# A shorter accumulating DMA with a fifth transpose group, later transposes in the first bodies, and a rearranged start in a fused dynamic convolution and two-matmul kernel

## The chip, the cores and the metric

One core of a Trainium2 chip runs the kernel. The metric is the device time of one execution in microseconds. Each run has a profile of one execution (its span is 1.7 to 2.1 us shorter than that execution's time) and, where rounds are given, repeated times beside the kernel before on the same chip. Three words recur. *Landing* is the moment at which all of a DMA's data is in place. The *slow clock* is a stretch in which the profile shows a granted TensorE clock of about half. A *one-off gap* is a stretch in which TensorE stands without waiting for anything that the profile names; where these gaps lie is told under e11.

## The reference, cut to what matters

```python
# attention part: x (8, 4096, 192), weight_gen (8, 4096, 8 heads, 7 taps)
w = exp(weight_gen - max); w = w / sum(w)          # softmax over the 7 taps
out[b,s,h,g] = sum_k w[b,s,h,k] * x[b, s-6+k, h*24+g]
# second part, on the 32768 x 192 result
h = x @ w_in          # 192 x 2048
g = h - tanh(h)
return g @ w_out      # 2048 x 192
```

## The kernel before

The kernel works on 32 blocks of 1024 tokens. For each block GpSimd multiplies x by the softmax weights, one product per tap, into three tiles: `even` (taps 0, 2, 4), `odd` (1, 3, 5) and `last` (6). An accumulating DMA adds `odd` to `even`. TensorE then transposes and adds up the four groups that are left (three of `even`, and `last`) by matmuls against an identity; ScalarE copies the result out of PSUM as `convT`.

```python
    def products(n, on_vector=()):
        ...
        for k in range(K):
            eng = nc.vector if k in on_vector else nc.gpsimd
            eng.tensor_mul(dst[k]..., x_t[:, k : k + J, :]..., wsm[:, :, :, k : k + 1]...)
            if k == K - 2:
                nc.gpsimd.dma_start(
                    out=even[:]..., in_=odd[:]...,
                    accum_op=mybir.AluOpType.add, max_dma_last_dim=3072)
        prods_of[n] = [even[:, i] for i in range(NPAIR)] + [last[:]]
```

The main loop interleaves, in program order of each engine, the two matmuls of neighbouring blocks with the transposes of the next block and the products of the block after that. A *body* is one pass of the outer loop, a *pair* one pass of the inner one.

```python
    for n in range(NTOT):
        if n + 3 < NTOT: load(n + 3)
        if n + 2 < NTOT: products(n + 2)
        for p in range(J):
            gemm1(n, 2 * p); gemm1(n, 2 * p + 1)      # tanh on ScalarE, subtraction on VectorE
            ...
            if n >= 1: gemm2((n - 1) * J + p)
            if n + 1 < NTOT:
                if p == (2 if n else 5): conv(n + 1, (0, 1))     # transposes of chunks 0 and 1
                if p == (5 if n else 6): conv(n + 1, (2,))       # and of chunk 2
            ...
```

The transposes use the same ring of three PSUM tiles as the first matmul (`tag="ph"`).

The softmax here doesn't subtract the row's maximum and nothing guards it: scores larger than these inputs give would overflow.

## Time and profile before

| what | before |
|---|---|
| time, first three runs | 808.31 us (807.36 to 809.03) |
| TensorE's body | 23.12 us |
| GpSimd's period | 22.74 us |
| accumulating DMA, issue to landing | 10.1 us |
| block 5: issue of its accumulating DMA / first transpose | 137.74 / 152.16 us |

Read it as two machines running in step: GpSimd with its DMA makes a block every 22.74 us, TensorE uses one every 23.12. The page's group rows give the unit costs. Columns: line, engine, operation, names, count, then busy us and mean ns of one, then idle time before them and its releasers:

```profile
L153 POOL TENSOR_TENSOR odd<-x_t,wsm 128x1536 bf16<-128x1536 f32 x92 | 268.5, 2919 | 0.0
L161 POOL DMA_DIRECT2D even<-odd x32 | 41.5, 1298 | 10.0 <-POOL odd L153 9.4
even<-odd POOLq DMA_DIRECT2D x32, 1152.0 KB, 10.1
```

A product costs GpSimd 2.9 us. Issuing the accumulating DMA costs it 1.30 us. The last row is of the DMA issues: 1152 KB each, 10.1 us from issue to landing.

### The profile page before, as it was taken

Reading aid. Unit: us, or ns where it says so; the run is one execution under the profiler, and the core shown is the slowest. Engines: PE = TensorE matmul, PEld = TensorE weight load, DVE = VectorE, ACT = ScalarE, POOL = GpSimd, SP = SyncE. Lnnn points to the kernel's source line nnn. Section 1 sums busy time; section 2 is a strip of 40 time slices with the busy share of each in tenths; the row PEclk is TensorE's granted clock in tenths of the full one; section 3 lists DMA queues with packets and bytes.
Section 4 is the critical chain, followed back from the end, with each engine's and each line's share of the span. In section 5 each row is a group of like instructions: output and inputs, shape, how many; then the busy total and the mean of one; then the engine's idle time right before and its main releaser. Section 6 shows DMA issues by size and latency. Waiting matters only on the chain.

```text
span 805.8 us, 31480 instructions
## 1 busy us (share of the span) xinstructions
PE 737.1 (91%) x14336; PEld 566.7 (70%) x14336; DVE 661.5 (82%) x591; ACT 643.4 (80%) x865; POOL 713.0 (88%) x297
## 2 busy tenths in 40 slices
PE   0066999999999999999999999999999999999997
PEld 0034777777777777777777777777777777777777
DVE  3867688888888888888888888888888888888883
ACT  0066788888888888888888888888888888888883
POOL 5999999999999999999999999999999999996000
PEclk9999999999999999999999999999999999999999
DMA  8794555676655655676565656775655667634112
GB/s 148 230 187 85 114 161 156 166 180 180 179 141 126 149 159 156 172 181 179 138 170 131 149 154 163 180 171 139 176 118 157 153 169 180 168 61 100 43 41 81
DMA packets 30068, 118.66 MB, mean 147 GB/s; under 512 B 4672, under 2 KB 9328, under 8 KB 25784
## 3 DMA queue, kind: packets, MB, share of 16 engines
q0 software_dynamic: 15376, 39.32, 30.6%
q1 hardware_dynamic: 14560, 77.34, 27.4%
q8 instruction: 112, 1.84, 0.9%
q14 instruction: 20, 0.16, 0.1%
HBM read 54.49 MB, written 25.17 MB: 99 GB/s over the span
## 4 chain that ended last, share of the span: by engine, by line
PE 76%; DVE 11%; POOL 5%; ACT 4%; DMA 3%; issue 1%; SPq 0%; POOLq 0%; DVEq 0%
PE ph L205 36%; PE po L236 35%; DVE gt L216 9%; ACT th L214 4%; PE pc L182 4%; POOL even L153 2%; POOL odd L153 2%; DMA x_t<-in_x_dram 1%; DVE odd L153 1%; PE po L277 1%; DMA even<-odd 1%; POOL last L153 0%; POOL wsm L137 0%; POOL even L161 0%; DVE even L153 0%
## 5 line engine op out<-in xcount | busy, mean ns | idle before, releaser
L216 DVE TENSOR_TENSOR gt<-ph,th 128x1024 bf16<-128x1024 f32 x512 | 602.8, 1220 | 106.7 <-ACT th L214 103.3
L214 ACT ACTIVATE th<-ph 128x1024 f32<-128x1024 f32 x512 | 500.3, 1022 | 64.0 <-PE ph L205 60.4
L205 PE MATMUL ph<-convT,w_in 64*128 64x512 bf16 x3072 | 391.9, 378 | 17.2 <-DVE gt L216 16.0
L236 PEld LDWEIGHTS <-gt 64*128 64x128 bf16 x7936 | 344.4, 94 | 52.8 <-ACT th L214 1.7
L236 PE MATMUL po<-w_out,gt 64*128 64x192 bf16 x7936 | 374.1, 243 | 1.7 <-ACT th L214 1.3
L153 POOL TENSOR_TENSOR even<-x_t,wsm 128x1536 bf16<-128x1536 f32 x95 | 281.8, 2967 | 14.2 <-DMA x_t<-in_x_dram 7.1
L153 POOL TENSOR_TENSOR odd<-x_t,wsm 128x1536 bf16<-128x1536 f32 x92 | 268.5, 2919 | 0.0
L205 PEld LDWEIGHTS <-w_in 64*128 64x128 bf16 x3072 | 170.3, 94 | 135.6 <-issue 44.9
L153 POOL TENSOR_TENSOR last<-x_t,wsm 128x1536 bf16<-128x1536 f32 x31 | 105.9, 3415 | 0.0
L261 ACT ACTIVATE out_sb<-po 128x192 f32<-128x192 f32 x248 | 82.0, 331 | 18.5 <-PE po L236 12.2
L192 ACT ACTIVATE convT<-pc 128x1024 bf16<-128x1024 f32 x64 | 51.7, 810 | 47.6 <-PE pc L182 43.5
L182 PE MATMUL pc<-ident,even 64*128 64x64 bf16 x2304 | 46.6, 193 | 45.9 <-DMA even<-odd 45.6
L182 PEld LDWEIGHTS <-even 64*128 64x128 bf16 x2304 | 43.7, 97 | 46.7 <-issue 46.4
L161 POOL DMA_DIRECT2D even<-odd x32 | 41.5, 1298 | 10.0 <-POOL odd L153 9.4
L137 POOL TENSOR_TENSOR wsm<-e_t,zr 128x448 f32<-128x448 f32 x32 | 46.3, 1446 | 0.0
L116 ACT ACTIVATE e_t<-wg_t 128x448 f32<-128x448 f32 x32 | 18.5, 578 | 20.3 <-DMA wg_t<-in_weight_gen_dram 20.3
L126 DVE TENSOR_REDUCE zsum<-e_t 128x64 f32<-128x448 f32 x32 | 19.5, 610 | 10.8 <-ACT e_t L116 10.8
L182 PE MATMUL pc<-ident,last 64*128 64x64 bf16 x768 | 23.4, 193 | 0.0
L153 DVE TENSOR_TENSOR odd<-x_t,wsm 128x1536 bf16<-128x1536 f32 x4 | 15.0, 3782 | 9.6 <-DMA x_t<-in_x_dram 9.6
L130 DVE RECIPROCAL zr<-zsum 128x64 f32<-128x64 f32 x32 | 17.7, 553 | 3.4 <-DVE zsum L126 0.5
L182 PEld LDWEIGHTS <-last 64*128 64x128 bf16 x768 | 17.3, 97 | 0.0
L277 PE MATMUL po<-w_out,gt 64*128 64x192 bf16 x256 | 11.0, 243 | 0.0
(15 smaller groups left out, 31.5 us busy)
## 6 DMA issues: line engine op xcount, KB each, us to landing
even<-odd POOLq DMA_DIRECT2D x32, 1152.0 KB, 10.1
x_t<-in_x_dram SPq DMA_DIRECT2D x24, 1344.0 KB
out_dram<-out_sb SPq DMA_DIRECT2D x31, 768.0 KB
x_t<-in_x_dram SPq DMA_DIRECT2D x8, 1176.0 KB
wg_t<-in_weight_gen_dram SPq DMA_DIRECT2D x32, 224.0 KB
x_t<-in_x_dram SPq DMA_DIRECT2D x8, 157.5 KB
w_in<-in_moe_w_in_dram POOLq DMA_DIRECT2D x8, 96.0 KB, 11.0
w_in<-w_in SPq DMA_DIRECT2D x1, 768.0 KB
```

Source lines behind the costliest of these rows:

```text
L126: nc.vector.reduce_sum(out=zsum[:], in_=e_t[:].rearrange("p j h k -> p (j h) k"), axis=AX.X)
L137: nc.gpsimd.tensor_mul(wsm[:].rearrange("p j h k -> p (j h) k"), e_t[:].rearrange("p j h k -> p (j h) k"), zr[:].rearrange("p (n o) -> p n ...
L153: eng.tensor_mul(dst[k].rearrange("p c j h g -> p j h c g"), x_t[:, k : k + J, :].rearrange("p j (h c g) -> p j h c g", h=H, c=NC), wsm[:, ...
L161: nc.gpsimd.dma_start(out=even[:].rearrange("p i c j h g -> p (i c j h g)"), in_=odd[:].rearrange("p i c j h g -> p (i c j h g)"), accum_o ...
L182: nc.tensor.matmul(pc[:, r, col : col + R], lhsT=prods[k][r * R : (r + 1) * R, c, 2 * j : 2 * j + 2].rearrange("p j h g -> p (j h g)"), rh ...
L192: nc.scalar.activation(out=convT[:, c0 : c0 + nch, :].rearrange("p c (j r t) -> p r (c j) t", r=2, t=R), in_=pc[:, :, 0 : nch * JH * R].re ...
L205: nc.tensor.matmul(ph[:, r, :], lhsT=w_in[r * R : (r + 1) * R, c, f * P : (f + 1) * P], rhs=convT[r * R : (r + 1) * R, c, :], start=(c == ...
L214: last_act[0] = nc.scalar.activation(out=th[:], in_=ph_f, func=ACT.Tanh)
L216: nc.vector.tensor_sub(gt[:], ph_f, th[:])
L236: mm = nc.tensor.matmul(po[:, 0:D], lhsT=g_of[n][f][r * R : (r + 1) * R, col : col + P], rhs=w_out[r * R : (r + 1) * R, f, :], start=(r == ...
L261: last_act[0] = nc.scalar.activation(out=out_sb[:, j, :], in_=po[:, 0:D], func=ACT.Copy)
L277: nc.tensor.matmul(po[:, r, 0:D], lhsT=g_of[n][f][r * R : (r + 1) * R, col : col + P], rhs=w_out[r * R : (r + 1) * R, f, :], start=(f == 0 ...
```

## The change

Its intent: shorten the start, in which TensorE has nothing to do, and keep TensorE from standing at the transposes of the first blocks. The accumulating DMA's row of 4608 elements per partition (3 runs of 1536 in the built kernel) is cut to 4096 (2 runs of 2048); the 512 elements left over become a fifth group of transposes for chunk 2.

```diff
+    ACC = NPAIR * J * D - J * R
...
                 nc.gpsimd.dma_start(
-                    out=even[:].rearrange("p i c j h g -> p (i c j h g)"),
-                    in_=odd[:].rearrange("p i c j h g -> p (i c j h g)"),
+                    out=even[:].rearrange("p i c j h g -> p (i c j h g)")[:, 0:ACC],
+                    in_=odd[:].rearrange("p i c j h g -> p (i c j h g)")[:, 0:ACC],
                     accum_op=mybir.AluOpType.add,
-                    max_dma_last_dim=3072,
+                    max_dma_last_dim=4096,
                 )
+            if k in hooks:
+                hooks[k]()
-        prods_of[n] = [even[:, i] for i in range(NPAIR)] + [last[:]]
+        groups = [even[:, i] for i in range(NPAIR)] + [last[:]]
+        prods_of[n] = [groups + ([odd[:, NPAIR - 1]] if c == NC - 1 else []) for c in range(NC)]
... (conv runs over a list of steps, with the fifth group for chunk 2 alone)
     load(0)
-    for h in range(H):
-        nc.gpsimd.dma_start(out=w_in[h * GC : (h + 1) * GC], ...)
     softmax_exp(0)
     softmax_norm(0)
-    products(0, on_vector=(1, 3, 5, 6))
-    nc.sync.dma_start(out=w_in[R:P], in_=w_in[0:R])
+    products(0, on_vector=(1, 3, 4, 5, 6), hooks={-1: load_w_in})   # w_in after wsm, copied in two halves
     load(1)
-    nc.gpsimd.dma_start(out=w_out[:], ...)
...
-    products(1, on_vector=(2, 5))
+    products(1, hooks={3: load_w_out})
...
-                if p == (2 if n else 5):
+                if p == (2 if n > 3 else 7):
                     conv(n + 1, (0, 1))
-                if p == (5 if n else 6):
+                if p == (5 if n > 3 else 7):
                     conv(n + 1, (2,))
```

Three parts will be told apart below: the *start*, the *DMA* (with its fifth group), and the *late transposes* (bodies 0 to 3).

More of the change, by code (lines that the diff above doesn't have):

```diff
@@ L131, in softmax_norm, with products @@
         zr_of[n] = (e_t, zr)
-    def products(n, on_vector=()):
+    def products(n, on_vector=(), hooks={}):
         x_t = x_of.pop(n)
@@ L150, in products @@
         dst[K - 1] = last[:]
+        if -1 in hooks:
+            hooks[-1]()
         for k in range(K):
@@ L176, in conv @@
         pc = psum_h.tile([P, 2, HT], FP32, name="pc", tag="ph")
-        for k in range(NPAIR + 1):
-            for ci, c in enumerate(chunks):
-                for j in range(JH):
-                    col = (ci * JH + j) * R
-                    for r in range(2):
-                        nc.tensor.matmul(
-                            pc[:, r, col : col + R],
-                            lhsT=prods[k][r * R : (r + 1) * R, c, 2 * j : 2 * j + 2].rearrange(
-                                "p j h g -> p (j h g)"
-                            ),
-                            rhs=ident[r * R : (r + 1) * R, r * R : (r + 1) * R],
-                            start=(k == 0 and ci == 0 and j == 0),
-                            stop=(k == NPAIR and ci == nch - 1 and j == JH - 1),
-                        )
+        steps = [
+            (gi, ci, c)
+            for gi in range(NPAIR + 2)
+            for ci, c in enumerate(chunks)
+            if gi < len(prods[c])
+        ]
+        for si, (gi, ci, c) in enumerate(steps):
+            for j in range(JH):
+                col = (ci * JH + j) * R
+                for r in range(2):
+                    nc.tensor.matmul(
+                        pc[:, r, col : col + R],
+                        lhsT=prods[c][gi][r * R : (r + 1) * R, c, 2 * j : 2 * j + 2].rearrange(
+                            "p j h g -> p (j h g)"
+                        ),
+                        rhs=ident[r * R : (r + 1) * R, r * R : (r + 1) * R],
+                        start=(si == 0 and j == 0),
+                        stop=(si == len(steps) - 1 and j == JH - 1),
+                    )
         c0 = chunks[0]
@@ L301, with load_w_out, load_w_in @@
     ctx.enter_context(tc.manual_schedule())
-    load(0)
-    for h in range(H):
-        nc.gpsimd.dma_start(
-            out=w_in[h * GC : (h + 1) * GC],
-            in_=moe_w_in[h * G : (h + 1) * G].rearrange("(c g) f -> g c f", c=NC),
-        )
+    def load_w_out():
+        nc.gpsimd.dma_start(out=w_out[:], in_=moe_w_out.rearrange("(c p) e -> p c e", c=NFT))
+    def load_w_in():
+        for h in range(H):
+            nc.gpsimd.dma_start(
+                out=w_in[h * GC : (h + 1) * GC],
+                in_=moe_w_in[h * G : (h + 1) * G].rearrange("(c g) f -> g c f", c=NC),
+            )
+        for q in range(2):
+            nc.sync.dma_start(
+                out=w_in[R + q * R // 2 : R + (q + 1) * R // 2],
+                in_=w_in[q * R // 2 : (q + 1) * R // 2],
+            )
+    load(0)
     softmax_exp(0)
     softmax_norm(0)
-    products(0, on_vector=(1, 3, 5, 6))
-    nc.sync.dma_start(out=w_in[R:P], in_=w_in[0:R])
+    products(0, on_vector=(1, 3, 4, 5, 6), hooks={-1: load_w_in})
     load(1)
-    nc.gpsimd.dma_start(out=w_out[:], in_=moe_w_out.rearrange("(c p) e -> p c e", c=NFT))
     softmax_exp(1)
```

## The prediction

> **What bounds the kernel now.** I read the page first (busy shares, the chain's shares), then the chain in order of time, then the timelines of GpSimd and TensorE up to 180 us, then busy time and DMA traffic by stretch.
>
> ```profile
> PE 737.1 (91%) x14336; PEld 566.7 (70%) x14336; DVE 661.5 (82%) x591; ACT 643.4 (80%) x865; POOL 713.0 (88%) x297
> PE 76%; DVE 11%; POOL 5%; ACT 4%; DMA 3%; issue 1%; SPq 0%; POOLq 0%; DVEq 0%
> ```
>
> Two engines are nearly full. TensorE carries the chain, but GpSimd's 88% is an average over a span in which it starts late and stops at 737 us, so it has hardly a gap while it works. The chain in order of time shows who hands over to whom:
>
> ```profile
> 69.52 10.52 DMA even<-odd
> 80.17 1.81 PE pc L182 x64
> 81.99 2.21 PE ph L205 x12
> ...
> 104.89 0.93 PE pc L182 x64
> 105.83 1.43 PE ph L205 x12
> ```
>
> Up to 80 us the chain is load, products on GpSimd and one accumulating DMA; from 80.17 on it is TensorE, with short passages through ScalarE and VectorE. The same 64 transposes take 1.81 us at 80.17 and 0.93 us at 104.89, and the 12 matmuls after them 2.21 against 1.43: TensorE had stood idle 3.62 us and ran slowly afterwards, which cost 0.88 + 0.78 = 1.7 us. Now the two rhythms, TensorE's transposes of chunks 0 and 1 and GpSimd's issues of the accumulating DMA:
>
> ```profile
> 80.17 1.39 PE L182 MATMUL pc<-ident,even 64*128 64x64 bf16 x48 [3.62 <-DMA even<-odd]
> ...
> 104.71 0.88 PE L182 MATMUL pc<-ident,even 64*128 64x64 bf16 x48
> ...
> 127.83 0.88 PE L182 MATMUL pc<-ident,even 64*128 64x64 bf16 x48
> ...
> 152.16 0.88 PE L182 MATMUL pc<-ident,even 64*128 64x64 bf16 x48
> ```
>
> ```profile
> 46.76 1.30 POOL L161 DMA_DIRECT2D even<-odd  x1 [0.30 <-POOL even L153]
> ...
> 69.52 1.30 POOL L161 DMA_DIRECT2D even<-odd  x1 [0.31 <-POOL odd L153]
> ...
> 137.74 1.30 POOL L161 DMA_DIRECT2D even<-odd  x1 [0.30 <-POOL odd L153]
> ```
>
> TensorE repeats every 23.12 us (104.71 to 127.83; the next step is 24.33 because of a 0.93 us gap marked "issue"). GpSimd repeats every 22.74 us ((137.74 - 69.52) / 3). GpSimd gains only about 0.4 us a body on TensorE. The issues at 46.76 and 137.74 serve blocks 1 and 5; at the median 10.1 us to landing, block 5 lands at 147.8, and TensorE asks for it at 152.16. The slack is 4.3 us. So TensorE bounds the steady state with GpSimd close behind, and any plan that moves TensorE earlier meets GpSimd's products after 4.3 us.
>
> The start:
>
> ```profile
> 14.68 10.51 DVE L153 TENSOR_TENSOR odd<-x_t,wsm 128x1536 bf16<-128x1536 f32 x3 [9.57 <-DMA x_t<-in_x_dram]
> ...
> 31.84 1.76 DVE L153 TENSOR_TENSOR even<-x_t,wsm 128x1536 bf16<-128x1536 f32 x1 [1.16 <-POOL wsm L137]
> 33.52 4.46 DVE L153 TENSOR_TENSOR odd<-x_t,wsm 128x1536 bf16<-128x1536 f32 x1
> ```
>
> ```profile
> 2.00:8.00 6.00, 0.00 (x0) 0.00 (x0) 1.17 (x2) 0.60 (x2) 5.48 (x10) 1.00 0.93 177
> 8.00:14.00 6.00, 0.00 (x0) 0.00 (x0) 0.00 (x0) 0.00 (x0) 0.00 (x0) 1.00 1.10 200
> 22.00:26.00 4.00, 0.00 (x0) 0.00 (x0) 4.00 (x2) 0.58 (x1) 4.00 (x2) 1.00 1.03 426
> 70.00:79.70 9.70, 5.25 (x85) 4.03 (x81) 6.77 (x7) 5.00 (x7) 9.62 (x5) 1.00 0.87 157
> ```
>
> The last two columns are the DMA engines' busy share and GB/s. The first x tile lands only at 14.6 us, because the casting load of w_in shares the engines (full from 2 to 14 us at under 200 GB/s). The second x tile, alone at 22 to 26, runs at 426 GB/s: 1.34 MB in about 3.5 us. VectorE's product takes 1.76 us when it goes first and 4.46 when it has to let one of GpSimd's (2.87) pass: the two alternate, they do not overlap.
>
> **What the Trainium skill says.** "DMA: Bandwidth & Descriptors", section "SDMA does more than copy": the in-line adder takes at most 2048 elements on trn2. The built kernels fit this: before splits its 4608 elements per partition into 3 runs of 1536, after its 4096 into 2 of 2048. No trace here shows the limit itself. "SBUF — State Buffer", section "Who interferes with whom": a VectorE instruction with two SBUF inputs and a GpSimd instruction that reads SBUF exclude each other for the whole instruction; the 1.76 and 4.46 us above agree (1.6 + 2.87 = 4.47). "TensorE: Matmul & The Clock Gate", Part 1: after an idle window of about 3.4 us TensorE's clock halves until it has been busy about as long; the 1.81 against 0.93 us after 3.62 us of idleness agrees.
>
> **The change part by part.**
>
> 1. w_in behind wsm. x tile 0 no longer shares the engines with w_in, whose issues now start at about 6.1 us (zr done 5.1, wsm 1.0). Tile 0 should land at about 8 to 10 instead of 14.6. GpSimd is then held by 8 issues of 0.6 us until 11.
>
> 2. Products(0), five on VectorE (1,3,4,5,6), two on GpSimd. VectorE starts at 8 to 10; then alternation: 2 x 2.87 + 5 x 1.6 = 13.7 us of exclusive time in all. Product 5 done at about 21 to 22, so DMA 0 is issued then instead of at 28.26. With a share of the engines going to x tiles it lands after some 12 us, near 34 instead of 42.0. Body 0 starts 8 us earlier.
>
> 3. Products(1) wholly on GpSimd. Takes back 2 x (2.87 - 1.6) = 2.5 us; the w_out issue (1.71 us in before, there in idle time) now lies in it. VectorE finishes block 0 at about 24, zsum and zr 1.2, wsm 1.0: start about 26.5, against 31.84. Then 7 - 1 = 6 products x 2.87 = 17.2, issue 1.7, wait 0.3: DMA 1 issued at about 46, against 46.76. The gain in the start is almost exactly spent; I set the shift of DMA 1 at -0.5 us, give or take 2.5.
>
> 4. Two thirds of the descriptors in each accumulating DMA. Landing: by bytes alone 8/9, by descriptors alone 2/3 of the roughly 8.5 us that the engines are full (0.87 x 9.7); I choose -1.5 us, 10.1 to 8.6. Issue on GpSimd: 384 descriptors 1.30 us, 24 descriptors (w_in) 0.61; estimate 1.05 us for 256. GpSimd's period becomes about 22.5.
>
> 5. The fifth group: 8 more transposes for chunk 2, i.e. 4 pairs; before, 16 such pairs take 0.46 us, so 0.12 us a block, 3.7 us over 32 blocks if all of it lay on the path. It does not from body 4 on: after these transposes TensorE waits 0.30 us for VectorE (row tiles at 92.29 and 115.40), since the transposes' tile took one of three PSUM buffers. I count it as absorbed.
>
> 6. Transposes last in bodies 0 to 3. Removes the 3.62 us stall in body 1 with its 1.7 us of slow clock. At a body's end the first matmul waits for ScalarE's copy of the transposes, about 0.8 us.
>
> TensorE's new schedule: body 0 from 37.5; + 19.5 = 57; conv(1) not waiting (46.2 + 8.7 = 55); body 1 from 59, body 2 from 84 (96.9 before), body 3 from 107, body 4 from 130; three pairs of 2.61 later, at 138, it asks for block 5. But block 5 lands at 46.2 + 4 x 22.5 + 8.6 = 144.8. TensorE stands 7 us there and then pays 1.6 us of slow clock. Before, the same transposes began at 152.16. Sum: 152.2 - 144.8 - 1.6 = 5.8 us gained, and from there on both kernels run at 23.12 us a body. 808.3 - 5.8 = 802.5 us.
>
> **The rivals.**
> - GpSimd does not hold TensorE (DMA 1 much earlier than 46). Then up to 96.9 - 84 = 13 us stay, 795 us. Against it: GpSimd's products are a fixed 2.87 us, and it cannot begin block 1 before block 0's VectorE share and zr are done.
> - The start moves the bottleneck to x tile 1. Its load now queues behind both w_in copies, which wait for a later w_in (about 18 us); if it lands at 29 to 30 instead of 26, DMA 1 slips to 48 or 49 and the gain falls to 2 or 3 us: 805.5.
> - The fifth group and the late transposes cost in every body: + 3.7 us, or more: then 806 to 808, a draw. For it: TensorE is the bound; against it: the 0.30 us waits.
> - The larger runs of the adder are slower per byte, landing beyond 10 us: block 5 lands at 147, gain 3 us.
>
> **Range and chances.** The dominant term is when block 5 lands, uncertain by about 3 us; next the fifth group, 0 to 3.7 us; last one-off gaps such as the 0.93 us one. Together about 3.5 us either way: 798 to 807. Two per cent is 16 us. Even the most favourable rival gives 13, so faster by over 2% has 2%; slower by over 2% needs an effect I see no sign of, 1%; within 2%, 97%.
>
> **What would show it.** Right: issue of the second accumulating DMA at 44 to 48 us and GpSimd's period near 22.5; landing under 9.2 us; no wait of TensorE on that DMA in body 1; instead one wait of 4 to 9 us for it in body 4, near 138 to 146 us, followed by transposes of about 1.8 us; from there 23.1 us a body. Wrong: no such wait (then the gain is larger); bodies of 23.3 us or more late in the run (the fifth group is on the path); GpSimd idle on x tile 1; an accumulating DMA as long as before.

## The result, and the profile after

The changed kernel took 804.12 us (803.36 to 805.08, 4 runs) against 808.13 us. The ratio is 0.9951, 95% interval 0.9933 to 0.9968. A second measurement on five more rounds gave 803.75 against 808.18, ratio 0.9949.

Of the profile after, first the page's busy row and the chain's shares. Nothing looks different; such shares cannot show this change:

```profile
PE 738.3 (92%) x14592; PEld 570.1 (71%) x14592; DVE 653.4 (82%) x590; ACT 644.2 (80%) x865; POOL 707.2 (88%) x298
PE 74%; DVE 13%; ACT 5%; DMA 4%; POOL 3%; issue 1%; SPq 0%; DVEq 0%; POOLq 0%; ACTq 0%
```

TensorE's timeline of the changed kernel (start, duration, work, and in brackets the idle time just before and what ended it):

```profile
82.86 0.88 PE L194 MATMUL pc<-ident,even 64*128 64x64 bf16 x48
...
85.09 1.53 PE L217 MATMUL ph<-convT,w_in 64*128 64x512 bf16 x12 [0.53 <-ACT convT L204]
...
96.96 0.82 PE L217 MATMUL ph<-convT,w_in 64*128 64x512 bf16 x6 [0.54 <-DVE gt L228]
...
106.77 0.88 PE L194 MATMUL pc<-ident,even 64*128 64x64 bf16 x48
...
139.48 1.50 PE L248 MATMUL po<-w_out,gt 64*128 64x192 bf16 x32
145.12 1.46 PE L194 MATMUL pc<-ident,even 64*128 64x64 bf16 x48 [4.14 <-DMA even<-odd]
```

The wait of body 1 is gone: block 2's transposes, at 82.86, wait for nothing. Instead TensorE stands 4.14 us at the first early place, body 4, for block 5. Bodies with late transposes take 23.91 us (82.86 to 106.77), 0.79 more than 23.12, with two waits of 0.53 us in them: for ScalarE's copy at the body's start, and for VectorE in the middle.

The start, GpSimd's timeline and then VectorE's:

```profile
6.24 4.84 POOL L320 DMA_DIRECT2D w_in<-in_moe_w_in_dram  x8
11.10 7.97 POOL L156 TENSOR_TENSOR even<-x_t,wsm 128x1536 bf16<-128x1536 f32 x2
22.95 1.28 POOL L165 DMA_DIRECT2D even<-odd  x1 [3.88 <-issue]
...
37.76 1.21 POOL L316 DMA_DIRECT2D w_out<-in_moe_w_out_dram  x1
...
45.07 1.21 POOL L165 DMA_DIRECT2D even<-odd  x1 [0.30 <-POOL odd L156]
```

```profile
10.17 6.14 DVE L156 TENSOR_TENSOR odd<-x_t,wsm 128x1536 bf16<-128x1536 f32 x2 [5.00 <-DMA x_t<-in_x_dram]
16.23 4.45 DVE L156 TENSOR_TENSOR even<-x_t,wsm 128x1536 bf16<-128x1536 f32 x1
20.61 1.74 DVE L156 TENSOR_TENSOR odd<-x_t,wsm 128x1536 bf16<-128x1536 f32 x1
```

The x tile is there at 10.1 instead of 14.6 us. The first accumulating DMA is issued 5.3 us earlier than before (22.95 against 28.26), the second only 1.7 us earlier (45.07 against 46.76): block 1's products, now all on GpSimd, give most of it back. Both figures are of single profiles, and the same code varies from run to run: the second accumulating DMA was issued at 45.22, 46.39 and 46.76 us with the old start (e1, e10, before) and between 45.05 and 46.32 us in the eight profiles with the new one and its block 1 unaltered. The means, 46.1 and 45.6, differ by 0.5 us only. The unit costs of the changed DMA:

```profile
L165 POOL DMA_DIRECT2D even<-odd x32 | 38.6, 1205 | 13.5 <-POOL odd L156 9.6
even<-odd POOLq DMA_DIRECT2D x32, 1024.0 KB, 8.9
```

**Where the 4.3 us between the two profiles came from.** Between 805.8 and 801.5 us the sum closes. Block 5's transposes begin 152.16 - 145.12 = 7.04 us earlier. Body 4 then takes 24.33 instead of 23.12 us (145.12 to 169.45): 1.2 us for the slow clock after the wait. Later bodies show one-off lengthenings of 0.15, 0.74, 0.17, 0.37 and 0.12 us, in all 1.55, where before shows none after block 5. 7.04 - 1.2 - 1.55 = 4.3. But before has its own gap just ahead of block 5, and 1.2 of the 7.04 us are that gap: its body from 127.83 to 152.16 took 24.33 us instead of 23.12.

```profile
130.85 0.81 PE L205 MATMUL ph<-convT,w_in 64*128 64x512 bf16 x5 [0.93 <-issue]
```

So two numbers describe each profile: when block 5's transposes begin, and how long the rest takes. The rest is at best 26 bodies of 23.12 us and an end of 52.6 us, 653.6 us in all (805.8 - 152.16); anything over that is slow clock and one-off gaps, up to 4.4 us below.

### The profile page after: what moved, and what is told of

It reads as the page before. It is cut to its first block, busy times and chain, and to the rows that moved or that the text cites. A ratio compares the mean times of both kernels' runs of the same rounds, so it can differ in the third digit from the quotient of the medians.

```text
span 801.5 us, 31993 instructions
## 1 busy us (share of the span) xinstructions
PE 738.3 (92%) x14592; PEld 570.1 (71%) x14592; DVE 653.4 (82%) x590; ACT 644.2 (80%) x865; POOL 707.2 (88%) x298
## 4 chain that ended last, share of the span: by engine, by line
PE 74%; DVE 13%; ACT 5%; DMA 4%; POOL 3%; issue 1%; SPq 0%; DVEq 0%; POOLq 0%; ACTq 0%
PE ph L217 35%; PE po L248 34%; DVE gt L228 11%; ACT th L226 4%; PE pc L194 4%; DMA even<-odd 3%; PE po L289 1%; POOL even L156 1%; POOL odd L156 1%; DMA x_t<-in_x_dram 1%; DVE odd L156 1%; POOL last L156 0%; ACT convT L204 0%; DVE even L156 0%; DVE zr L131 0%
## 5 line engine op out<-in xcount | busy, mean ns | idle before, releaser
L156 POOL TENSOR_TENSOR even<-x_t,wsm 128x1536 bf16<-128x1536 f32 x95 | 277.9, 2925 | 7.6 <-POOL wsm L138 6.1
L165 POOL DMA_DIRECT2D even<-odd x32 | 38.6, 1205 | 13.5 <-POOL odd L156 9.6
L138 POOL TENSOR_TENSOR wsm<-e_t,zr 128x448 f32<-128x448 f32 x32 | 44.5, 1392 | 5.1 <-DVE zr L131 5.1
L156 DVE TENSOR_TENSOR odd<-x_t,wsm 128x1536 bf16<-128x1536 f32 x3 | 7.9, 2654 | 5.0 <-DMA x_t<-in_x_dram 5.0
```

What stands on the lines that cost most here:

```text
L138: nc.gpsimd.tensor_mul(wsm[:].rearrange("p j h k -> p (j h) k"), e_t[:].rearrange("p j h k -> p (j h) k"), zr[:].rearrange("p (n o) -> p n ...
L156: eng.tensor_mul(dst[k].rearrange("p c j h g -> p j h c g"), x_t[:, k : k + J, :].rearrange("p j (h c g) -> p j h c g", h=H, c=NC), wsm[:, ...
L165: nc.gpsimd.dma_start(out=even[:].rearrange("p i c j h g -> p (i c j h g)")[:, 0:ACC], in_=odd[:].rearrange("p i c j h g -> p (i c j h g)" ...
```

## The experiments

In the table, "block 5" is when its transposes of chunks 0 and 1 begin, and "rest" is the span from there to the end. The changed kernel's first measurement has four runs of each kernel, e1 to e11 are of five rounds. The median of before was 807.00 us in the rounds of e1 to e4, 808.18 in those of e5 to e8 and 807.65 in those of e9 to e11, so ratios compare better across these sets than medians. The 95% intervals reach 0.0012 to 0.0019 to either side: e1, e2, e3 and e10 are not told apart from one another. The shorter DMA with its fifth group alone was not run.

| run | median us | ratio to before | block 5 | rest |
|---|---|---|---|---|
| before (profile above) | 808.13 | 1 | 152.16 | 653.6 |
| changed kernel | 804.12 | 0.9951 | 145.12 | 656.4 |
| e5, changed kernel again | 803.75 | 0.9949 | 146.35 | 657.1 |
| e1, late transposes alone | 805.87 | 0.9978 | 147.54 | 656.1 |
| e9, start alone | 806.77 | 0.9991 | 151.70 | 653.8 |
| e2, start and DMA | 805.09 | 0.9969 | 149.33 | 653.7 |
| e3, start and late transposes | 805.11 | 0.9969 | 145.86 | 657.6 |
| e10, DMA and late transposes | 805.70 | 0.9975 | 146.09 | 658.0 |
| e4, one product more in block 1 | 807.35 | 0.9997 | 148.93 | 656.5 |
| e6, VectorE helps in block 1 | 799.63 | 0.9895 | 143.08 | 654.6 |
| e8, more of it, late to body 2 | 798.68 | 0.9885 | 140.75 | 655.7 |
| e7, late to body 6 | 805.58 | 0.9959 | see text | see text |
| e11, no stores | 804.86 | 0.9959 | 145.19 | 655.2 |
| e12, four runs (one look) | 805.15 | not timed | 146.91 | 656.4 |

The theory: the landing of block 5's products, fixed by GpSimd's chain from the start on, decides when TensorE's steady rhythm begins. (With the transposes at their old places, in before, e2 and e9, TensorE meets that same chain earlier, at block 2, and does not wait at block 5.) Rivals: TensorE itself is the bound and the late transposes make the gain; or the start and the DMA make it and the late transposes only cost; or the fifth group costs in each body.

**e1: the late transposes alone, on the kernel before.**

```diff
-                if p == (2 if n else 5):
+                if p == (2 if n > 3 else 7):
-                if p == (5 if n else 6):
+                if p == (5 if n > 3 else 7):
```

> The kernel before with the late transposes (last in bodies 0 to 3) and nothing else of the change. My theory (block 5's landing sets when the steady rhythm starts, about 147.8 us here): body 0 starts at 45 as before, TensorE asks for block 5 some 103 us later, at about 148, and waits for it less than 1 us, without a slow clock; the transposes of block 5 begin near 148.2 instead of 152.2, so 4 us gained: about 804, as fast as the whole change. Rival (the earlier start and the shorter accumulating DMA make the gain, late transposes only cost their 0.8 us a body): 808 or more.

Measured 805.87 us, ratio 0.9978. The wait for block 5 is short, as expected:

```profile
147.54 0.97 PE L182 MATMUL pc<-ident,even 64*128 64x64 bf16 x48 [1.17 <-DMA even<-odd]
```

Block 5 begins 4.6 us earlier than before (1.2 of them are the gap in the profile of before), with no slow clock at the transposes (0.97 us). But 2.4 us of one-off gaps follow, and half of the expected 4 us is left. The rival (808 or more) falls: late transposes do not merely cost.

**e2: the changed kernel with the transposes at their old places** (the reverse of e1's edit).

> The changed kernel with the transposes at their old places. My theory: TensorE waits for block 2 in body 1 (lands near 76.7) for 5 to 7 us, pays the slow clock there, and then runs three bodies of 23.1 us to block 5 at about 147.5, after its landing at 145.0, with no second wait. Against 145.1 plus 1.5 of slow clock in the changed kernel this is 1 us later: about 805, so most of the gain stays. Rival (the late transposes make the gain): back at 808.

Measured 805.09 us, ratio 0.9969. The expected wait is in body 1:

```profile
76.07 1.47 PE L194 MATMUL pc<-ident,even 64*128 64x64 bf16 x48 [5.63 <-DMA even<-odd]
```

No wait for block 5 follows, but block 5 comes at 149.33 instead of 147.5, because 2.1 us of gaps fell between blocks 3 and 5. Most of the gain stays without the late transposes, so they are not its only source either.

**e3: the changed kernel with the old accumulating DMA and no fifth group.**

```diff
-    ACC = NPAIR * J * D - J * R
+    ACC = NPAIR * J * D
-                    max_dma_last_dim=4096,
+                    max_dma_last_dim=3072,
-        prods_of[n] = [groups + ([odd[:, NPAIR - 1]] if c == NC - 1 else []) for c in range(NC)]
+        prods_of[n] = [groups for c in range(NC)]
```

> The changed kernel with the accumulating DMA over all 4608 elements in 3 runs of 1536 and no fifth group. My theory: landing 10.1 us instead of 8.9 and GpSimd's period 22.74 instead of 22.64, so block 5 lands 1.5 us later, the wait in body 4 grows from 4.1 to about 5.6 us and the time by 1.5: about 805.5; the steady body stays at 23.12. Rival (the fifth group lies on TensorE's path): up to 3.7 us faster than the changed kernel, 800.5, with shorter bodies.

Measured 805.11 us, ratio 0.9969. The landing is 10.1 us and GpSimd's period 22.74 again (113.28 to 136.02), and block 5 begins 0.7 us later than in the changed kernel, not 1.5: block 5's own DMA landed in 9.7 us. The wait was 2.96 us, not 5.6, because TensorE itself arrived later in this run: its first body began 1.8 us later. The fifth group's rival falls. The steady body is 23.12 us here without it and in the changed kernel with it, though the group itself is there:

```profile
L194 PE MATMUL pc<-ident,odd 64*128 64x64 bf16 x256 | 9.7, 192 | 0.0
```

That row is of the changed kernel; its busy time is in places where TensorE waited anyway: from the start of chunk 2's transposes to the next matmul of the first product it is 0.58 us both before (161.14 to 161.72) and after (155.31 to 155.89).

**e4: one product of block 1 computed twice on GpSimd.**

```diff
-            eng.tensor_mul(
+            for _ in range(2 if n == 1 and k == 0 else 1):
+              eng.tensor_mul(
```

> The changed kernel with one product of block 1 computed twice on GpSimd (2.86 us more before the second accumulating DMA, same result). My theory: block 5 lands 2.9 us later, the wait in body 4 grows from 4.1 to 7.0 us, the whole time by 2.9: about 807. Rival (TensorE bounds, GpSimd has slack): no change, 804.

Measured 807.35 us, ratio 0.9997: 3.2 us over the changed kernel in medians (of other rounds; by the two ratios about 3.7), and practically the whole gain is gone. GpSimd has no slack there. Block 5:

```profile
148.93 1.47 PE L195 MATMUL pc<-ident,even 64*128 64x64 bf16 x48 [4.02 <-DMA even<-odd]
```

The wait grew less than expected (4.02, not 7.0), since a one-off gap of 2.42 us in body 2 had delayed TensorE; but the transposes began 3.8 us later all the same. Of these 3.8 us, 2.9 are the product and the rest the later start of this run (first accumulating DMA at 23.81 instead of 22.95).

**e5: the changed kernel again**, beside the next three.

> The changed kernel once more, so that it shares its runs of before with the next three. Every theory: about 4 us under before, with the wait for block 5 of about 4 us near 141 to 145.

803.75 us against 808.18, ratio 0.9949; wait 4.15 us, block 5 at 146.35. GpSimd's line, then TensorE's:

```profile
46.32 1.21 POOL L165 DMA_DIRECT2D even<-odd  x1 [0.30 <-POOL odd L156]
```

```profile
146.35 1.46 PE L194 MATMUL pc<-ident,even 64*128 64x64 bf16 x48 [4.15 <-DMA even<-odd]
```

The wait agrees to 0.01 us with the first profile, the absolute times differ by 1.2 us from the start on. The price of the wait does not agree: the next body took 25.75 us here and 24.33 there, so the slow clock cost 2.6 against 1.2 us (granted clock 0.50 from 147 to 151 us here).

**e6: products 1, 3 and 5 of block 1 on VectorE.**

```diff
-    products(1, hooks={3: load_w_out})
+    products(1, on_vector=(1, 3, 5), hooks={3: load_w_out})
```

> The changed kernel with products 1, 3 and 5 of block 1 on VectorE, which is idle then (25 to 39 us). My theory: GpSimd and VectorE alternate, three pairs of 4.47 us instead of 6 x 2.87 + 1.2 for the w_out issue, so the second accumulating DMA is issued near 40 instead of 45 and block 5 lands at about 140, before TensorE asks for it at 141: no wait in body 4, no slow clock, transposes of block 5 at 141 instead of 145.1 and 1.5 us less after it: 5.6 us under the changed kernel. Rival (the second accumulating DMA is not what the end hangs on): equal to the changed kernel.

Measured 799.63 us, ratio 0.9895: 4.1 us under the changed kernel of the same rounds. GpSimd's timeline, then TensorE's line:

```profile
27.38 8.85 POOL L156 TENSOR_TENSOR even<-x_t,wsm 128x1536 bf16<-128x1536 f32 x2
36.17 1.21 POOL L316 DMA_DIRECT2D w_out<-in_moe_w_out_dram  x1
37.40 3.21 POOL L156 TENSOR_TENSOR even<-x_t,wsm 128x1536 bf16<-128x1536 f32 x1
40.91 1.21 POOL L165 DMA_DIRECT2D even<-odd  x1 [0.31 <-POOL even L156]
```

```profile
143.08 0.88 PE L194 MATMUL pc<-ident,even 64*128 64x64 bf16 x48 [1.04 <-DMA even<-odd]
```

The second accumulating DMA is issued at 40.91 instead of 46.32 (e5). GpSimd had 5.4 us less to do and TensorE got 3.3 of them: the wait fell from 4.15 to 1.04 us and the slow clock with it (granted clock 1.00 from 141 to 147 us). The last 1 us of wait came from this one DMA landing after 11.45 us where e5's took 9.31. This is the clearest support of the theory: nothing on TensorE was touched.

**e7: late transposes up to body 6.**

```diff
-                if p == (2 if n > 3 else 7):
+                if p == (2 if n > 6 else 7):
-                if p == (5 if n > 3 else 7):
+                if p == (5 if n > 6 else 7):
```

> The changed kernel with the transposes late in bodies 0 to 6 instead of 0 to 3. My theory: each late body takes 23.9 us against GpSimd's 22.64, so the wait at the switch shrinks by 1.3 us a body; in body 7 TensorE asks at 212.7 and block 8 lands at about 212.9: no wait and no slow clock, 3 us under the changed kernel. Rival (late bodies simply add 0.8 us each): 2.4 us over it.

Measured 805.58 us, ratio 0.9959: a miss, 1.8 us over the changed kernel of the same rounds in medians, 0.8 in means; the two intervals overlap. Its five times fall in two groups (803.22 and 804.20; 805.58, 805.75 and 805.80), and the profile is of the slower one. The wait went as expected:

```profile
214.26 0.88 PE L194 MATMUL pc<-ident,even 64*128 64x64 bf16 x48 [0.27 <-DMA even<-odd]
...
242.25 0.29 PE L194 MATMUL pc<-ident,last 64*128 64x64 bf16 x4 [2.47 <-issue]
```

Block 8 was met at 214.26 with hardly a wait. With three bodies of 23.12 back that equals block 5 at 144.9, without a slow clock at the switch. But the next two bodies took 24.46 and 27.07 us. The second line shows one cause: 2.47 us in which TensorE waited for nothing that the profile shows, and the slow clock after it. In this profile the expected gain was given back in such gaps.

**e8: products 1, 3, 4 and 5 of block 1 on VectorE, late transposes in bodies 0 to 2.**

```diff
-    products(1, hooks={3: load_w_out})
+    products(1, on_vector=(1, 3, 4, 5), hooks={3: load_w_out})
-                if p == (2 if n > 3 else 7):
+                if p == (2 if n > 2 else 7):
-                if p == (5 if n > 3 else 7):
+                if p == (5 if n > 2 else 7):
```

> The changed kernel with products 1, 3, 4 and 5 of block 1 on VectorE and the transposes late in bodies 0 to 2 only. My theory: second accumulating DMA issued near 39, block 4 lands at about 116.3, TensorE asks for it in body 3 at 116.9: no wait, one late body of 0.8 us fewer: 6.5 us under the changed kernel, the fastest so far. Rival as in the run with three products on VectorE.

Measured 798.68 us, ratio 0.9885, the fastest of all: 5.1 us under the changed kernel of the same rounds, 1.4 less than expected. There is no wait for an accumulating DMA after block 0. The rest (655.7) again contains 2.1 us over the ideal.

**e9: the start alone** (e3's edit and e2's together).

> The new start alone (loads, shares of VectorE in blocks 0 and 1, w_out delayed), with the old accumulating DMA and the transposes at their old places. My theory: TensorE asks for block 2 in body 1 near 71 and gets it at about 78, pays the slow clock, then 24.5 + 2 x 23.1 us to block 5 at about 148.7, after its landing at 146.2: 3.5 us under before, about 804.5. Rival (the start's gain is fully spent by block 1's products on GpSimd): 808.

Measured 806.77 us, ratio 0.9991, interval 0.9979 to 1.0004: not told apart from no gain at all. The wait in body 1 is there:

```profile
78.63 1.46 PE L194 MATMUL pc<-ident,even 64*128 64x64 bf16 x48 [6.14 <-DMA even<-odd]
```

Before waited 3.62 us and went on at 80.17, so the earlier start of TensorE turned into 2.5 us more of waiting, and 1.5 us remained at block 2. By block 5 only 0.5 is left: 0.7 us went in the slow clock after the longer wait (a body of 25.26 against 24.54 us) and 0.4 in the body before block 5 (24.69 us, with a gap of 1.28, against 24.33 in before, with its gap of 0.93). The expected 804.5 is missed; the rival's reading, that the start's gain is spent by block 1's products on GpSimd, is nearer.

**e10: the old start with the shorter DMA, the fifth group and the late transposes.**

```diff
     load(0)
+    load_w_in()
...
-    products(0, on_vector=(1, 3, 4, 5, 6), hooks={-1: load_w_in})
+    products(0, on_vector=(1, 3, 5, 6))          # w_in copied in one piece, w_out loaded after load(1)
...
-    products(1, hooks={3: load_w_out})
+    products(1, on_vector=(2, 5))
```

> The old start with the shorter accumulating DMA, the fifth group and the late transposes. My theory: the second accumulating DMA is issued near 46 as in the other kernels, block 5 lands at 145 to 146, TensorE asks for it at about the same time, so no slow clock: transposes of block 5 near 146, as good as the changed kernel (145.1 and 1.2 us of slow clock): about 804. Rival (the whole change needs its new start): 806 or more.

Measured 805.70 us, ratio 0.9975. Block 5 begins at 146.09 without a wait and without a slow clock, right as expected, and 0.3 us before that of e5. Yet the rest is 658.0: 4.4 us of one-off gaps. Where TensorE stands at block 5 the new start adds nothing; the total is inconclusive about more, because the gaps are as large as what is sought. With all of the change the ratio is 0.9951 and 0.9949; whether the remaining 0.0025 belongs to the new start or to such gaps (here 1.70 us at 151 us and 0.85 at 198 us), no run separates.

**e11: no stores of blocks 0 to 30** (wrong result; the store is deleted). This was to find the cause of the gaps.

> The changed kernel without the stores of blocks 0 to 30 (wrong result on purpose): 24 of 114 MB of DMA traffic less. Theory of the one-off gaps of TensorE (0.4 to 2.5 us, each near the end of a stretch in which the DMA engines are full, no shown cause): something that TensorE needs comes late by DMA; with shorter full stretches the gaps after the switch, 1.5 to 1.9 us in the two profiles of the changed kernel, fall below 0.8 us and the time by about 1 us. Rival: gaps and time as in the changed kernel, 803.8. Block 5 lands as before.

Inconclusive. In the profile the bodies after body 4 lengthen by only 0.18 us in all (1.55 in the changed kernel), as the theory had it. But the five times are 802.16, 805.21, 802.39, 804.86 and 805.07: two groups, and the ratio, 0.9959, is not better than the changed kernel's 0.9949. The profiled run fell in the lower group. This run does not settle the cause of the gaps.

The traces do show where the gaps lie. TensorE's own instructions also come by DMA: the queue that the profile calls "instruction" moved 112 packets of 16384 bytes in before and 114 in the changed kernel, which is one for every 256 of TensorE's 28672 and 29184 matmuls and weight loads. Between 80 and 760 us the fourteen traces hold 23 gaps of 0.36 to 2.47 us: 22 that the timeline marks "issue", and one (e1, at 174.80) that it puts down to VectorE's `zr`, which that matmul does not read. All 23 stand at the boundary of two such groups of 256 (counted in the trace, with a slip of one instruction per body), and 21 of them end 1.26 to 1.63 us after the packet of that group landed (the other two 0.75 and 0.88). At the other boundaries, some 1300, TensorE was at the median 4.3 us behind the landing. So in a gap TensorE stands, as far as the trace tells, for its next 256 instructions. The same boundary (after 21 groups) has the gap in the changed kernel, e4, e5, e6, e10 and e12: 0.59, 1.16, 0.44, 0.42, 0.85 and 0.61 us. So these gaps are not mere chance; they go with how a kernel's instruction stream falls on its DMA traffic. Why a packet comes late, and whether moving a boundary removes its gap, no run tested.

**e12: 4096 elements in four runs of 1024.**

```diff
-                    max_dma_last_dim=4096,
+                    max_dma_last_dim=2048,
```

> The changed kernel with the same 4096 elements in 4 runs of 1024 instead of 2 of 2048. If the number of runs sets the landing (3 runs 10.1, 2 runs 8.9 us): 11 us or more. If the bytes do: 8.9. From both, as I think: about 9.4. The issue on GpSimd: 1.30 us for 384 descriptors and 1.21 for 256 make 1.39 for 512.

```profile
L165 POOL DMA_DIRECT2D even<-odd x32 | 41.6, 1301 | 14.0 <-POOL odd L156 10.1 <-issue 3.9
even<-odd POOLq DMA_DIRECT2D x32, 1024.0 KB, 8.9
```

The landing is 8.9 us, as with two runs: at the median the landing went by the bytes, not by the runs (10.1 x 4096 / 4608 = 9.0), though block 5's own DMA took 9.88 us here and 9.34 in the changed kernel. The issue took 1.30 us for 512 descriptors (128 partitions of 4 runs), the same as for 384 before, and 1.21 for 256: it does not go up in proportion, and my 1.39 was wrong.

## Why the prediction was right, point by point

The prediction was 802.5 us with a range of 798 to 807; measured were 804.1 and 803.8.

- **What bounds it.** Right: the changed kernel shows the one wait foretold, in body 4 for block 5. The prediction had the landing at 144.8; TensorE's transposes followed it at 145.12. e4 and e6 confirm the cause by moving GpSimd's work in both directions.
- **Part 1, w_in behind wsm.** Right, at the edge: the x tile was there at 10.1 us (8 to 10 foretold).
- **Part 2, products of block 0.** Right within 1 us in this profile: first accumulating DMA at 22.95 (21 to 22; up to 24.2 in others), landing at 34.6 (34).
- **Part 3, products of block 1.** Right: second accumulating DMA at 45.07, 1.1 us earlier than foretold, of which 0.5 is the w_out issue (1.21 us, not 1.7). Over all profiles the new start moves it by the -0.5 us foretold.
- **Part 4, the DMA.** Landing 8.9 (8.6 foretold, of which I had put too much on the number of runs); issue 1.21 us, not 1.05, so GpSimd's period is 22.64, not 22.5. Over four periods that is 0.6 us, and block 5's own DMA took 9.34 us, 0.7 more than foretold. Together they undo the 1.1 us of part 3. So that block 5 landed within 0.2 us of the foretold 144.8 (45.07 + 4 x 22.64 + 9.34 = 145.0) is luck: three misses cancelled.
- **Part 5, the fifth group.** Right: bodies of 23.12 us with and without it.
- **Part 6, the late transposes.** The end of the body costs ScalarE's 0.53 us, as foretold in kind, but another 0.53 us appears before VectorE, and a late body takes 23.91 us. TensorE therefore came at 141.0, not 138. That did not matter to the time, since it waited there in any case: the wait was 4.1 instead of 7 us.
- **The sum.** Foretold 5.8 us, measured 4.3 in the profile. The difference is not in the 7.04 us by which block 5 came earlier (7.4 foretold) nor in the slow clock (1.2, 1.6 foretold). It is the claim that from there on both kernels run at 23.12 us a body: 1.55 us of one-off gaps followed. I had named such gaps in the range, but counted none for the changed kernel and left before's own, 1.2 us, in the 152.2 that I subtracted from. Without gaps on either side the same sum gives 4.6 us. e2 and e9, which like before transpose early, have a gap at the same boundary (0.70 and 1.28 us), so it may well belong to that kernel; only one profile of before was kept.
- **The rivals.** "GpSimd does not hold TensorE" fell by the wait itself. "The bottleneck moves to x tile 1" fell: GpSimd's products of block 1 do not wait for it. The fifth group in every body fell by e3. "Larger runs are slower" fell by 8.9 us.

## What to carry to other kernels

When two engines run in step at nearly the same period (here 22.64 and 23.12 us), starting the consumer (TensorE) earlier only moves its wait to the first place where it meets the producer (GpSimd); look for the landing that it cannot overtake, and shorten the chain to that landing. Here three idle slots of VectorE in block 1 were worth as much again as the whole change (e6: 8.5 us under before by medians, the change 4.4). And where the looked-for gain is 2 to 4 us in 800, compare where a marked instruction begins in the trace as well as the total: one-off gaps, up to 4 us together, blur the latter. Such a gap need not be noise: count the engine's instructions up to it before calling it chance.

## What the Trainium skill lacked or had wrong

- "TensorE: Matmul & The Clock Gate", Part 1, gives an idle window of about 3.4 us before the slow clock. In these runs the slow clock came after idle times of 2.42 us (e4: granted clock 0.50 from 88 to 90 us) and 2.96 us (e3: granted clock 0.50 from 148 to 150 us, body of 24.59 us) and did not come after one of 3.32 us (e12: granted clock 1.00 from 144 to 152 us, body of 23.12 us). The page says that the window runs free, which allows the 3.32; the 2.42 and 2.96 it does not state. After the wait for block 5 the price was 1.2 us in the changed kernel and 2.6 in e5, the same kernel.
- "DMA: Bandwidth & Descriptors" gives no duration for an accumulating DMA within the on-chip memory. Here 1.0 MB took 8.9 us and 1.15 MB 10.1 us from issue to landing, and 2 or 4 runs per partition made no difference (e12).
- The same page calls descriptor generation on GpSimd small and variable. Here the issue took 1.21 us for 256, 1.30 us for 384 and 1.30 us for 512 descriptors, once per 22.6 us period.
- "Runtime: NRT & Kernel Launch", section "Instruction fetch mechanics", says that an engine's instructions are refilled in blocks of 256 by a DMA queue of its own, and calls the cost of crossing a block mostly hidden. The packet counts here agree (112 for 28672 instructions). The cost was not hidden in the 23 gaps of 0.36 to 2.47 us (before: 0.93 us at 130 us; e7: 2.47 us at 240 us), which all stand at such a boundary. Many lay near the ends of stretches with full DMA engines; that is a coincidence in time, and e11 did not settle whether these delay the blocks.
